# Attention and a gated feed-forward on one core: input products by blocks of seven, weights streamed from DRAM

## The chip, the cores and the metric

The kernel runs on one core of one Trainium2 chip. A core has TensorE (PE, with its weight loads shown apart as PEld), VectorE (DVE), ScalarE (ACT), GpSimd (POOL) and SyncE (SP), which here issues DMAs. The metric is the device time of one execution in microseconds; lower is better.

## The reference

```python
# q, k, v: (B=8, H=8, S=576, D=64); w_a, w_b: (512, 1536); w_out: (1536, 512); all float32
k_p = k.reshape(B, H, 72, 8, D).mean(axis=3)          # keys and values pooled by 8
v_p = v.reshape(B, H, 72, 8, D).mean(axis=3)
scores = (1 / sqrt(D)) * q @ k_p^T
attn = softmax(scores) @ v_p
x = attn.transpose(0, 2, 1, 3).reshape(4608, 512)     # one row a token
out = ((x @ w_a) * (x @ w_b)) @ w_out
```

## The kernel before

**Precision.** TensorE is given operands rounded to `fp32r`. To keep float32 accuracy each operand is split in a high part (a copy that rounds) and a low part (the rest, `low_part`, L172), and each product is three matmuls: high by high, high by low, low by high. The weights arrive as 64-bit words (`words`), which `convert_weights` turns into float32 with two ACT and three DVE operations a block (L212 to L223).

**Work.** The feed-forward runs over 9 tiles of 512 tokens (`NT`) and, in each, over 12 blocks of 128 hidden units (`f`). For a block `ffn_in` makes two products into PSUM (`psa`, `psb`; 4 blocks of the model width x 3 matmuls of 512 columns each, L549 to L551); ACT copies the first out (L554), DVE multiplies the second by it (L527), and the result is split (`hh`, `hl`). `ffn_out` multiplies it by `w_out` into four PSUM tiles `acc` (L570 to L572), which gather over all 12 blocks and are written out once a tile (L576, L578). The float32 weights stay in SBUF (`raw`, 72 KB in each partition); `split_weight` splits each block anew for every tile: one ACT copy (L235) and one low part, on DVE in tile 0 for `a` and `b`, on POOL otherwise.

**Attention** goes in 40 chunks of up to 128 tokens (`chunk`): load of queries, split, scores (L389 in the first `SUMMED` chunks, L403 and L406 later, with L409 adding two halves), softmax, split of the probabilities, transposes (L474) and, for a block of chunks, the product with the values (L507 to L510), whose result is split into `xh` and `xl`, the feed-forward's input.

**Order.** Nothing reorders at run time: each engine follows the order in which the program emits. `Chains` holds generators; each yields the number of steps until it goes on, or `PE` for a place between feed-forward matmuls. `ffn_in` and `ffn_out` call `chains.step()` between their groups, so attention, splits and conversions are laid between the products; `need` steps until something has been emitted. All DMAs go out on SP in program order, so a DMA that waits holds up those behind it.

Of the kernel before, what the change touches and what calls it, by code (L numbers as in the profile page):

```python
# [23 lines left out]
NT = 512  # L24
NTILE = B * S // NT
NF = DF // P
NK = DM // P


SHRINK = 2.0**-112  # L30
SCALE = 1.0 / float(D) ** 0.5
# [11 lines left out]


# [5 lines left out]
SLOTS = 6  # L50
TILE_SLOTS = SLOTS * NF

BLOCK, BLOCK_LATER = 256, 384

NTMP = 6

SUMMED = 9

AHEAD = 2

GROUPS = 4


SPLIT_A, SPLIT_B, SPLIT_O = 1, 4, 4
PROBS_GAP, VALUE_GAP = 2, 4
CHUNK, CHUNK_LATER, CHUNK_GAP = 34, 32, 10
KEYS_AHEAD, VALUES_AFTER = 18, 16


EARLY_GAP, VALUES_START, KEYS_START, WEIGHTS_START, CONVERT_AFTER = 1, 2, 4, 10, 5  # L70
# [3 lines left out]

# [35 lines left out]

@with_exitstack
def attn_moe_kernel(ctx: ExitStack, tc: tile.TileContext, q, k, v, vr, wa, wb, wo, out):
# [15 lines left out]
    raw = {name: const.tile([P, NF, 512], F32, name=f"w{name}_raw") for name in ("a", "b", "o")}
# [8 lines left out]
    work = sb.tile([P, 2 * NK * BLOCK_LATER], I32, tag="work", name="words", bufs=1)  # L140
    area = {name: work[:, x * 1024:(x + 1) * 1024] for x, name in enumerate(("a", "b", "o"))}

    flat = [(b, o, n) for b in range(B) for o, n in chunks_of(b)]
    tile_of = [(b * S + o) // NT for b, o, n in flat]
    early = sum(t == 0 for t in tile_of)

    blocks, start = [], 0

    def cut(chunks, limit):

        best = None
        for x in range(1, len(chunks) + 1):
            total = sum(flat[c][2] for c in chunks[:x])
            if total > limit:
                break
            cost, rest = cut(chunks[x:], limit) if x < len(chunks) else (0, [])
            cost += max(total, 2 * P)
            if best is None or cost < best[0]:
                best = cost, [chunks[:x]] + rest
        return best  # L160

    while start < len(flat):
        stop = start
        while stop < len(flat) and flat[stop][0] == flat[start][0] and tile_of[stop] == tile_of[start]:
            stop += 1
# [19 lines left out]
    def load_early():  # L185
# [7 lines left out]
        for i in range(2, early):  # L193
            load_raw_queries(i, early_q[:, i])
# [488 lines left out]
```

## Time and profile before

| | |
|---|---|
| runs | 1088.93, 1089.23, 1089.97 us; median 1089.23 |
| span of the profiled execution, first to last instruction | 1086.9 us; its whole time is not listed apart from the runs, and the median stands 2.3 us above the span |
| busy: PE, PEld, DVE, ACT, POOL | 1029.8, 856.0, 580.4, 523.3, 531.7 us |
| granted TensorE clock | 0.984 of full over the span |
| DMA | 59.58 MB, 55 GB/s on average |
| first feed-forward product, end of tile 0, of tile 1, start of the last tile | 58.6, 203, 313.4, 982.2 us |

Matmuls are pipelined, and a matmul's recorded duration overlaps the next one's: 512 columns are listed at 0.39 us and start 0.23 us apart. Rows of groups give line, engine, operation, output <- inputs, shapes and count, then busy us and mean ns of one, then idle time of the engine just before them and what ended it.

### The profile page before, as it was taken

How to read it: one execution, taken by the hardware profiler on the slowest of the kernel's cores; microseconds unless marked ns; L12 is line 12 of the kernel's file. 1: busy time of each engine (PE TensorE's matmuls, PEld its weight loads, DVE VectorE, ACT ScalarE, POOL GpSimd, SP SyncE). 2: the span in 40 equal slices, each digit the busy share in tenths (PEclk: the TensorE clock that was granted, in tenths of full speed). 3: DMA queues.
4: the chain of work that ended last, by engine and by line, in shares of the span. 5: the costliest groups of instructions: out<-in, count | busy, mean ns of one | idle time of the engine just before them, and what ended most of it. 6: DMA issues, size and time to landing. Idle time of an engine off the chain costs nothing.

```text
span 1086.9 us, 13596 instructions
## 1 busy us (share of the span) xinstructions
PE 1029.8 (95%) x4964; PEld 856.0 (79%) x4964; DVE 580.4 (53%) x941; ACT 523.3 (48%) x1051; POOL 531.7 (49%) x441
## 2 busy tenths in 40 slices
PE   4388779999999999999999999999999999999998
PEld 4277667888887888888888888888888888888886
DVE  8889998733476335733476436644457243322112
ACT  3666566544454445544455445444445344443332
POOL 6112322555545554665555555555546455555442
PEclk9779989999999999999999999999999999999999
DMA  6454453200121001400040003100221020001001
GB/s 222 134 157 129 134 169 110 89 23 1 56 84 46 2 3 44 129 1 1 22 131 1 1 1 120 55 1 1 73 73 30 1 68 1 1 1 39 1 1 39
DMA packets 29874, 59.58 MB, mean 55 GB/s; under 512 B 7121, under 2 KB 7121, under 8 KB 29809
## 3 DMA queue, kind: packets, MB, share of 16 engines
q1 hardware_dynamic: 29808, 58.73, 16.9%
q8 instruction: 39, 0.64, 0.2%
q14 instruction: 27, 0.21, 0.1%
HBM read 49.28 MB, written 9.44 MB: 54 GB/s over the span
## 4 chain that ended last, share of the span: by engine, by line
PE 84%; DVE 9%; ACT 3%; DMA 2%; issue 1%; POOL 0%; SPq 0%; DVEq 0%; ACTq 0%; POOLq 0%
PE acc L570 9%; PE psa L549 9%; PE acc L572 8%; PE psa L551 8%; PE acc L571 8%; PE psb L549 8%; PE psa L550 8%; PE psb L551 8%; PE psb L550 8%; PE ptr L474 3%; PE psc L403 2%; DVE wb_raw L218 1%; PE po L509 1%; PE po L510 1%; PE psc L406 1%
## 5 line engine op out<-in xcount | busy, mean ns | idle before, releaser
L527 DVE TENSOR_TENSOR h<-psb,h 128x512 f32<-128x512 f32 x108 | 74.5, 690 | 343.7 <-PE psb L551 326.6
L172 POOL TENSOR_TENSOR jlb<-wb_raw,jhb 128x512 fp32r<-128x512 f32 x96 | 125.6, 1309 | 218.2 <-ACT jhb L235 218.2
L172 POOL TENSOR_TENSOR jla<-wa_raw,jha 128x512 fp32r<-128x512 f32 x96 | 126.5, 1317 | 140.9 <-ACT jha L235 117.9
L172 POOL TENSOR_TENSOR jlo<-wo_raw,jho 128x512 fp32r<-128x512 f32 x108 | 154.2, 1428 | 82.4 <-ACT jho L235 74.8
L554 ACT COPY h<-psa 128x512 f32<-128x512 f32 x108 | 63.5, 588 | 234.7 <-PE psa L551 229.4
L570 PE MATMUL acc<-jho,hh 128*128 128x512 f32 x432 | 174.3, 404 | 0.0
L549 PE MATMUL psb<-xh,jhb 128*128 128x512 f32 x432 | 171.6, 397 | 1.9 <-DVE h L527 1.9
L549 PE MATMUL psa<-xh,jha 128*128 128x512 f32 x432 | 172.5, 399 | 0.0
L551 PE MATMUL psb<-xh,jlb 128*128 128x512 f32 x432 | 169.4, 392 | 0.1
L572 PE MATMUL acc<-jho,hl 128*128 128x512 f32 x432 | 169.3, 392 | 0.0
L551 PE MATMUL psa<-xh,jla 128*128 128x512 f32 x432 | 169.2, 392 | 0.0
L550 PE MATMUL psa<-xl,jha 128*128 128x512 f32 x432 | 169.2, 392 | 0.0
L571 PE MATMUL acc<-jlo,hh 128*128 128x512 f32 x432 | 169.1, 391 | 0.0
L550 PE MATMUL psb<-xl,jhb 128*128 128x512 f32 x432 | 168.9, 391 | 0.0
L530 ACT CAST hh<-h 128x512 fp32r<-128x512 f32 x108 | 67.1, 622 | 76.7 <-DVE h L527 76.7
L172 DVE TENSOR_TENSOR hl<-h,hh 128x512 fp32r<-128x512 f32 x108 | 91.6, 848 | 20.8 <-ACT hh L530 20.6
L551 PEld LDWEIGHTS psb<-xh,jlb 128*128 128x128 f32 x432 | 81.6, 189 | 18.0 <-DVE jlb L172 0.6
L551 PEld LDWEIGHTS psa<-xh,jla 128*128 128x128 f32 x432 | 81.7, 189 | 17.7
L572 PEld LDWEIGHTS acc<-jho,hl 128*128 128x128 f32 x432 | 81.4, 188 | 17.7
L549 PEld LDWEIGHTS psb<-xh,jhb 128*128 128x128 f32 x432 | 81.5, 189 | 17.5 <-issue 2.3
L429 POOL TENSOR_TENSOR s<-s,z 128x576 f32<-128x576 f32 (+1 forms) x38 | 52.3, 1376 | 86.3 <-DVE z L427 48.8
L549 PEld LDWEIGHTS psa<-xh,jha 128*128 128x128 f32 x432 | 81.7, 189 | 15.3
(91 smaller groups left out, 1721.6 us busy)
## 6 DMA issues: line engine op xcount, KB each, us to landing
out<-y SPq DMA_DIRECT2D x36, 256.0 KB, 2.2
kraw<-in_k SPq DMA_DIRECT2D x28, 288.0 KB, 3.5
vraw<-in_v SPq DMA_DIRECT2D x28, 256.0 KB, 3.0
qraw<-in_q SPq DMA_DIRECT2D x28, 256.0 KB, 3.7
words<-in_wa SPq DMA_DIRECT2D x12, 512.0 KB, 3.6
words<-in_wb SPq DMA_DIRECT2D x12, 512.0 KB, 3.5
words<-in_wo SPq DMA_DIRECT2D x12, 512.0 KB, 3.6
vraw<-in_vr SPq DMA_DIRECT2D x14, 192.0 KB, 2.6
```

The costliest lines, as they stand in the source:

```text
L172: eng.tensor_tensor(out=lo, in0=src, in1=hi.bitcast(F32), op=ALU.subtract)
L429: (nc.vector if first and i % 2 else nc.gpsimd).tensor_tensor(out=s[:n], in0=s[:n], in1=z[:n].unsqueeze(2).broadcast_to([n, H, SP]), op=AL ...
L474: nc.tensor.transpose(ptr[:rows, g, :n], src, ident[:n, :n])
L527: nc.vector.tensor_tensor(out=h, in0=pt, in1=h, op=ALU.mult)
L530: nc.scalar.copy(hh, h)
L549: nc.tensor.matmul(pt, wh[:, c], xh[:, kk], start=(kk == 0), stop=False)
L550: nc.tensor.matmul(pt, wh[:, c], xl[:, kk], start=False, stop=False)
L551: nc.tensor.matmul(pt, wl[:, c], xh[:, kk], start=False, stop=(kk == NK - 1))
L554: nc.scalar.copy(h, pt)
L570: nc.tensor.matmul(acc[c], hh[:, cs], wh, start=(f == 0), stop=False)
L571: nc.tensor.matmul(acc[c], hh[:, cs], wl, start=False, stop=False)
L572: nc.tensor.matmul(acc[c], hl[:, cs], wh, start=False, stop=(f == NF - 1))
```

## The change

**Blocks of seven.** Tokens are taken in pairs of halves of 384 (`HB`): 6 pairs of 768. Pair 0 is done as before, with matmuls of 384 columns. From pair 1 on, `block` takes a pair of hidden blocks (`j`: hidden blocks 2j and 2j+1), the two halves of the model width and the two token halves as 2x2 matrices and makes the product from seven block products instead of eight (`PRODUCTS7`), for `w_a` and `w_b` (m = 0, 1) each. Products gather in four PSUM banks, X and Y for each matrix; between products that use the same bank ACT copies a partial result out (`snap`) or DVE adds it to one taken before (`combine`). The left factors are parts of the weights or sums of them (S1 to S4), the right ones blocks of x or sums of them (T1 to T4).

**Weights.** They no longer stay in SBUF. While pair 0 runs, each block is converted (two ACT and two DVE operations now; the words are loaded from ACT's DMA queue), split once, used, and its parts stored to DRAM (`keep`), the float32 block too. `block_sums` loads that back, makes the four sums on POOL, splits and stores them. From then on `load_parts` streams each item's seven left factors and two blocks of `w_out` from DRAM, 512 KB each, into rings of SBUF buffers (`own`, `stream`, `raws`, `outs`). A `Ring` hands out a buffer only when the program has emitted the last use of its earlier content.

**Output.** `outer` makes the output product of one item (two hidden blocks) into one of two PSUM tiles; `taken_outer` copies the first into SBUF and adds the later ones there with DVE. Items of pair 0 are ordered so that j = 0, 1 come first for half 0 alone, then j = 2 to 5 for both halves, then j = 0, 1 for half 1 (`LEAD` = 2).

**Attention** of pair p + 1 is spread over the items of pair p and leaves x unsplit in `xraw`; `prepare` forms and splits the seven right factors while the last item of pair p goes through. The early steps take three chunks instead of four, and the shorter score path holds for 14 chunks instead of 9.

The diff, cut to its core:

```diff
-NT = 512
+NJ = NF // 2
+HB = 384
+NP = 2 * HB
+PRODUCTS7 = (
+    ("A11", "B11", "X", True), ("A12", "B21", "Y", True), ("S2", "T2", "X", False), ("S1", "T1", "Y", True),
+    ("S3", "T3", "X", False), ("S4", "B22", "Y", False), ("A22", "T4", "X", False),
+)
-SUMMED = 9
+SUMMED = 14
+BLOCK_STEPS = 20
+raws = Ring(sb, "raw", 3, [P, 2, 512], F32)
+own = Ring(sb, "we", 4, e_shape, F32R)
+stream = Ring(sb, "ws", 4, e_shape, F32R)
+outs = Ring(sb, "wo", 4, [P, 2, 512], F32R)
+gates = Ring(sb, "h", 7, [P, HB], F32)
+gated = Ring(sb, "hh", 6, [P, 2, HB], F32R)
+    def keep(key, e, ring, after=STORE_AFTER):
+        yield after
+        kept[key] = dr.tile([P, 1024], F32, name="kept_%s_%s" % key)
+        nc.sync.dma_start(kept[key], flat_e.bitcast(F32))
...
+            nc.scalar.activation(w, hi.bitcast(F32), AF.Copy, scale=SHRINK)
+            nc.scalar.activation(low, lo.bitcast(U32), AF.Copy, scale=LOW_BITS)
+            if f + 2 < NF:
+                load_words(f + 2)                      # nc.scalar.dma_start
-            nc.vector.tensor_scalar(...); nc.vector.scalar_tensor_tensor(...); nc.vector.tensor_tensor(...)
+            nc.vector.scalar_tensor_tensor(
+                out=low, in0=wi, scalar=3, in1=low, op0=ALU.logical_shift_left, op1=ALU.bitwise_or)
+            nc.vector.scalar_tensor_tensor(
+                out=wi, in0=wi, scalar=-(1 << 31), in1=low, op0=ALU.bitwise_and, op1=ALU.bitwise_or)
+    def split_inner():
...
+                nc.scalar.copy(e[:, 0], src)
+                low_part((nc.vector, nc.gpsimd)[h], e[:, 1], src, e[:, 0])
+                chains.start(keep((f, h), e, None), LATER, 1)
+            chains.start(keep(("raw", f), rawt[f], raws), LATER, 1)
+    def block_sums(j):
...
+            nc.sync.dma_start(r[-1].rearrange("p m c -> p (m c)"), kept["raw", f])
+        for name, a, b, op in (S1, S2, S4, S3):
+            nc.gpsimd.tensor_tensor(out=t, in0=a, in1=b, op=op)
+            while not own.can():
+                yield 1
+            e = own.take((j, name))
+            nc.scalar.copy(e[:, 0], t)
+            low_part(nc.gpsimd, e[:, 1], t, e[:, 0])
+            chains.start(keep((j, name), e, own), LATER, 1)
+    def load_parts():
+        while len(loaded) < len(wanted) and wanted[len(loaded)] in kept:
+            x = len(loaded)
+            ring = stream if x < first_block else (own, stream)[x % 2] if x < first_third else (own, stream, raws)[x % 3]
+            if not ring.can():
+                break
+            e = ring.take(x, e_shape, F32R)
+            nc.sync.dma_start(e..., kept[wanted[x]])
+    def block(item):
+        for x, (left, right, bank, opens) in enumerate(PRODUCTS7):
+            need(lambda: len(loaded) > taken["i"] and ("operand", p, right) in done)
+            for m in range(2):
+                need(lambda: ("read", name) in done or (name, "open") not in done)
+                for kk in range(2):
+                    nc.tensor.matmul(pt, e[:, 0, m, c], xo[:, 0, kk], start=(opens and kk == 0), ...)
+                    nc.tensor.matmul(pt, e[:, 0, m, c], xo[:, 1, kk], ...)
+                    nc.tensor.matmul(pt, e[:, 1, m, c], xo[:, 0, kk], ...)
+                chains.start(taken_block(item, x, m, pt, name, snaps), PRODUCTS, 1)
+                step()
+            if x: yield                                # once for each m; one group of outer() goes here
+        # taken_block: snap = ACT copy of the bank to SBUF; combine = DVE add of bank and snap, then for m = 1
+        # POOL multiplies the two matrices' results, ACT rounds, POOL makes the low part
+    def outer(item):
+        for half in halves(item):                      # (1, 0)
+            for c in range(HB // P):
+                pt = ps.tile([P, DM], F32, tag="acc", bufs=2)
+                for y in range(2): three matmuls of 512 columns
+    def taken_outer(item, row, tokens, pt):
+        if opens: nc.scalar.copy(acc[row], pt)
+        else: nc.vector.tensor_tensor(out=acc[row], in0=pt, in1=acc[row], op=ALU.add)
+items = [("n", (0,), j) for j in range(LEAD)] + [("n", (0, 1), j) for j in range(LEAD, NJ)]
+items += [("n", (1,), j) for j in range(LEAD)] + [("s", p, j) for p in range(1, NPAIR) for j in range(NJ)]
+        for x in range(NJ):
+            chains.start(behind(begins["s", 1] + (x - 2) * BLOCK_STEPS, block_sums(x)), LATER)
```

More of the change, by code (lines that the diff above doesn't have):

```diff
@@ new lines, in split_outer @@
+    def split_outer():
+        for f in range(NF):
+            yield from wait(("weight", "o", f))
+            while not outs.can() or order_o[next_o[0]] != ("own", f):
+                yield 1
+            next_o[0] += 1
+            e = outs.take(("own", f))
+            w = rawt.pop(("o", f))
+            nc.scalar.copy(e[:, 0], w)
+            yield 1
+            low_part(nc.gpsimd, e[:, 1], w, e[:, 0])
+            tmps.give(("o", f))
+            parts["o", f] = e
+            chains.start(keep(("o", f), e, None), LATER, 1)
+            yield 2
@@ new lines, in attn_moe_kernel, with step, need, finish @@
+    taken = {"i": 0, "o": 0}
+    def step(groups=1):
+        chains.step(groups)
+        load_parts()
+    def need(ready):
+        n = 0
+        while not ready():
+            step(GROUPS)
+            n += 1
+            assert n < 2000
+    acc = {}
+    gs = {}
+    def finish(key, f, half, h):
+        while not gated.can():
+            yield 1
+        e = gated.take((key, f, half))
+        nc.scalar.copy(e[:, 0], h)
+        yield 1
+        low_part(nc.gpsimd, e[:, 1], h, e[:, 0])
+        gates.give((key, f, half))
+        gs[key, f, half] = e
@@ new lines, in taken_outer @@
+    def taken_outer(item, row, tokens, pt):
+        j = item[2]
+        opens, closes = j == 0, j == NJ - 1
+        if item[0] == "n" and row >= HB // P:
+            opens, closes = j == LEAD, j == LEAD - 1
+        if opens:
+            acc[row] = sb.tile([P, DM], F32, tag=f"acc{row}", name=f"y_{tokens}", bufs=1)
+            nc.scalar.copy(acc[row], pt)
+        else:
+            nc.vector.tensor_tensor(out=acc[row], in0=pt, in1=acc[row], op=ALU.add)
+        if closes:
+            yield 1
+            nc.sync.dma_start(out[tokens:tokens + P, :], acc[row])
+        else:
+            return
+            yield
@@ new lines, in attn_moe_kernel, with behind @@
+        need(lambda: have(0) and ("parts", 0) in done)
+        begins, starts, at = {}, [], 0
+        for item in items:
+            begins.setdefault(item[:2], at)
+            starts.append(at)
+            at += BLOCK_STEPS if item[0] == "s" else 11 * len(item[1])
+        def behind(when, chain):
+            x = max(y for y in range(len(starts)) if starts[y] <= when)
+            yield from wait(("item", x))
+            if when > starts[x]:
+                yield when - starts[x]
+            yield from chain
@@ L638 @@
+        step()
+        step()
+        for _ in before:
+            step()
+        for _ in range(4):
+            step()
 _OUTS = [((B * S, DM), "float32")]
```

675 lines of the change are left out of this document (477 added, 198 removed).

## The prediction

> **What bounds the kernel now.** I read the page's engine shares first, then the table of windows cut at the first product and at the borders of token tiles, then single matmuls in the timeline.
>
> ```profile
> span 1086.9 us, 13596 instructions
> ...
> PE 1029.8 (95%) x4964; PEld 856.0 (79%) x4964; DVE 580.4 (53%) x941; ACT 523.3 (48%) x1051; POOL 531.7 (49%) x441
> ...
> PE 84%; DVE 9%; ACT 3%; DMA 2%; issue 1%; POOL 0%; SPq 0%; DVEq 0%; ACTq 0%; POOLq 0%
> ...
> 0.00:58.60 58.60, 25.57 (x120) 23.18 (x121) 48.35 (x83) 28.56 (x61) 23.00 (x33) 0.87 0.56 182
> 58.60:203.00 144.40, 124.19 (x589) 99.59 (x588) 131.19 (x211) 89.01 (x177) 38.85 (x29) 0.94 0.41 129
> 203.00:313.40 110.40, 110.40 (x537) 92.70 (x536) 50.65 (x86) 52.02 (x105) 59.84 (x48) 1.00 0.12 41
> 313.40:982.20 668.80, 668.80 (x3279) 557.35 (x3279) 329.83 (x535) 319.76 (x649) 366.98 (x298) 1.00 0.11 35
> 982.20:1086.90 104.70, 100.84 (x445) 83.15 (x444) 20.34 (x28) 33.90 (x61) 42.97 (x34) 1.00 0.06 21
> ```
>
> The window columns are PE, PEld, DVE, ACT, POOL, then granted clock, DMA share, GB/s. There are two kernels in one. Until 203 us (attention of tile 0, then tile 0's products beside the weight conversion) DVE is busy 131.2 of 144.4 us: DVE is the limit. From 203 us PE never pauses and the others are half idle; six tiles take 668.8 us, 111.5 each. How dense PE is there the timeline says (start, duration):
>
> ```profile
> 316.16 0.39 PE L549 MATMUL psb<-xh,jhb 128*128 128x512 f32 x1
> ...
> 318.65 0.39 PE L551 MATMUL psb<-xh,jlb 128*128 128x512 f32 x1
> ...
> 718.73 0.34 PE L507 MATMUL po<-p,vdiag 128*128 128x384 f32 x1
> 718.90 0.34 PE L508 MATMUL po<-p,vdiag 128*128 128x384 f32 x1
> 719.09 0.34 PE L509 MATMUL po<-p,vdiag 128*128 128x384 f32 x1
> 719.26 0.34 PE L510 MATMUL po<-p,vrem 96*128 96x384 f32 x1
> 719.44 0.40 PE L570 MATMUL acc<-jho,hh 128*128 128x512 f32 x1
> ```
>
> Start to start, 11 matmuls of 512 columns take 2.49 us, 0.2265 each; four of 384 take 0.71, 0.1775 each, with a weight load for each matmul as everywhere. Three quarters of 0.2265 is 0.170: the narrower matmul is not held up by its weight load, it pays 0 to 0.0075. I take 0.176. A tile's 432 products of 512 columns are 97.9 us, so attention costs PE 13.6 a tile.
>
> **Steady part: block items.** An item is 768 tokens by 256 of the hidden width, both matrices. Before, that is 72 matmuls of 512 columns: 16.3 us. After, 7 products x 2 matrices x 6 matmuls of 384: 84 x 0.176 = 14.8. Saved 1.5 an item, 46 over 30 items (bounds 43 to 61). Pair 0 stays unblocked but at 384: 96 x 0.176 = 16.9 an item, 0.6 lost, 3.5 in six. The output products stay 36 x 0.2265 = 8.2 an item. So an item is 23.0 us, a pair 138, with attention for the next pair (1.5 x 13.6) 158.
>
> The Trainium skill, "TensorE: Matmul & The Clock Gate", section "Back-to-back issue gap", gives N/2.4 + 2.5 ns for warm matmuls, so 162.5 and 215.8 ns for these widths. By it the estimate is 56 us saved over 30 items instead of 46; the rows above are 5 to 9% slower than the page, and I go by the rows.
>
> What an item adds elsewhere is priced by these groups (busy, mean ns):
>
> ```profile
> L527 DVE TENSOR_TENSOR h<-psb,h 128x512 f32<-128x512 f32 x108 | 74.5, 690 | 343.7 <-PE psb L551 326.6 <-PE ptr L474 6.2 <-ACT qh L358 6.0
> ...
> L172 DVE TENSOR_TENSOR xl<-po,xh 128x384 fp32r<-128x384 f32 x16 | 8.9, 554 | 7.8 <-ACT xh L518 7.8
> ...
> L518 ACT CAST xh<-po 128x384 fp32r<-128x384 f32 x16 | 7.7, 478 | 16.9 <-PE po L510 16.9
> ...
> L172 POOL TENSOR_TENSOR jlo<-wo_raw,jho 128x512 fp32r<-128x512 f32 x108 | 154.2, 1428 | 82.4 <-ACT jho L235 74.8 <-DVE jla L172 7.6
> ...
> L172 POOL TENSOR_TENSOR jlb<-wb_raw,jhb 128x512 fp32r<-128x512 f32 x96 | 125.6, 1309 | 218.2 <-ACT jhb L235 218.2
> L172 DVE TENSOR_TENSOR hl<-h,hh 128x512 fp32r<-128x512 f32 x108 | 91.6, 848 | 20.8 <-ACT hh L530 20.6
> ...
> L235 ACT CAST jho<-wo_raw 128x512 fp32r<-128x512 f32 x108 | 67.2, 622 | 0.0
> ...
> 605.32 0.39 PE L551 MATMUL psa<-xh,jla 128*128 128x512 f32 x1
> ...
> 605.75 0.59 ACT L554 COPY h<-psa 128x512 f32<-128x512 f32 x1 [1.20 <-PE psa L551]
> ```
>
> DVE: seven combinations out of PSUM at 0.554 and, because an output product no longer stays in PSUM over twelve hidden blocks but is added up in SBUF after each item, six additions at 0.690: 8.0 an item, 48 a pair. Attention on DVE is 55 a tile less 12 x (0.690 + 0.848) for gates, 36, so 54 a pair; preparing the next pair's operands (4 sums, 4 low parts of 768 columns) 9. Sum 111 of 158, 70%, against 49% before. ACT: 53 a tile less 36 splits at 0.622 and 24 gate copies at 0.6 leaves 16 for attention, 24 a pair; eleven copies at 0.48 an item, 32; seven 768-wide copies and six first output rows, 10: 66 of 158. POOL: seven ops of about 1.07 (three quarters of 1.428), 45 a pair, plus attention (367/6 less 36 splits at 1.36, the mean of the two rows, = 12 a tile, 18) and three low parts of 768 columns, 6: 69 of 158. No engine passes PE on average. What is tight is order. The X bank that product 7 leaves is opened again by the next item after only six matmuls, 1.06 us, and the copy must read it between: 0.2 from the matmul's end to the copy's start (an estimate: 605.75 - 605.32, less the 0.2265 that the matmul streams) and 0.48, or 0.55 on DVE. An engine inside another op then makes PE wait 0.3 to 0.6. The output product also waits for DVE, POOL, ACT and POOL in a row (0.55 + 1.07 + 0.5 + 1.07, before hops) in a 5.2 us space. I charge 0.7 an item, 4 a pair (bounds 0 and 2.5).
>
> **Streams.** Per item SP issues seven block loads and two output-weight loads, 512 KB each, 4.7 MB; with q, k, v and results 222 GB/s through the pair. SP's own time, about 0.4 per issue by the chain's two rows below, is 3.6 of 26 us. A load that waits for a buffer to be freed holds up the q, k, v loads and the result stores behind it on SP, and attention would wait for them; query chunks start 34 steps early (an item is 20), so nothing is charged.
>
> ```profile
> 0.74 0.37 SPq L183
> 1.16 0.42 SPq L188
> ...
> words<-in_wo SPq DMA_DIRECT2D x12, 512.0 KB, 3.6
> ...
> 0.00:27.00 27.00, 12.96 (x56) 11.86 (x56) 22.04 (x38) 9.37 (x20) 18.29 (x28) 1.00 0.67 221
> ...
> 135.00:162.00 27.00, 21.20 (x105) 17.44 (x104) 25.20 (x43) 16.93 (x34) 6.45 (x5) 0.88 0.51 163
> ```
>
> 221 GB/s at share 0.67 and 163 at 0.51 both extrapolate to some 325: 222 is 68% of it, with up to 11 buffers (1.6 items) ahead. Hidden.
>
> **Pair 1** has the block sums besides: per item four sums and four low parts on POOL, 8 x 1.36 = 11, four copies on ACT, two reloads and four stores on SP. POOL goes to 45 + 18 + 6 + 65 = 134 of 158, 85%, and a sum has to be made, stored and reloaded (3.6 each way) before its product. Its buffers come from the ring that the loads also use. No row shows such a chain; bounds 0 and 60 for the pair, I take 12, nearer the first since each chain starts two items ahead.
>
> **Start.** To the end of pair 0, three engines compete.
>
> ```profile
> L223 DVE CUSTOM_DVE_ANT_0 wb_raw<-wb_raw,wlow_b 128x1024 uint16<-128x1024 uint16 x12 | 11.7, 971 | 1.5
> L218 DVE SCALAR_TENSOR_TENSOR wb_raw<-words,wb_raw 128x512 int32<-128x512 int32 x12 | 11.3, 943 | 0.2
> ...
> L214 DVE TENSOR_SCALAR wb_raw<-wb_raw 128x512 int32<-128x512 int32 x12 | 6.3, 522 | 2.9 <-ACT wb_raw L212 2.9
> ...
> L172 DVE TENSOR_TENSOR jlb<-wb_raw,jhb 128x512 fp32r<-128x512 f32 x12 | 8.2, 681 | 0.0
> ...
> L409 DVE TENSOR_REDUCE s<-psc 128x144 f32<-128x288 f32 x100 | 41.1, 451 | 54.0 <-PE psc L406 53.6
> L374 DVE TENSOR_TENSOR s<-s,m 128x576 f32<-128x576 f32 x25 | 28.3, 1133 | 0.9
> ...
> L373 DVE TENSOR_REDUCE m<-s 128x8 f32<-128x576 f32 x25 | 18.8, 752 | 0.8
> ...
> L374 DVE TENSOR_TENSOR s<-psc,m 128x288 f32<-128x288 f32 x14 | 6.4, 457 | 0.9
> L373 DVE TENSOR_REDUCE m<-psc 128x4 f32<-128x288 f32 x14 | 6.3, 448 | 0.4 <-PE psc L389 0.4
> ```
>
> DVE did 48 + 131 us of work until 203, and half of 51 more until 768 tokens were through, at about 258: 205. Three conversion ops become two of L218's kind: about 0.55 x 36 = -20. Half of the 24 early low parts (0.68 to 0.77) and 18 gate low parts (0.848) leave for POOL: -9, -15. 30 output additions: +21. 256 more tokens of attention must be done by then: +18. Five more chunks take the shorter score path, 2 x (0.457 + 0.448) instead of 4 x 0.451 + 1.133 + 0.752, and pair 1's x gets no low part there: -11. Preparation +9. Sum 198; at the 91% of before, 218. PE: first product at about 53 (58.6 before, with four chunks instead of three ahead of it), 101 + 49 us of products, 30 of attention: 233. DMA: 12 x 7 transfers of 512 KB (three words, four stores) and 6 MB of inputs, 50 MB at 325 GB/s, 154 us in the 190 there are; words are now issued on ACT (36 x 0.4, hidden in 60% use). Three limits this close add waits: I take 245 (bounds 228 and 270).
>
> **Sum.** 245, pair 1 158 + 4 + 12, pairs 2 to 4 3 x 162, pair 5 (no attention behind it) 142, end 3.8 as now plus 3 for the last output product, which has nothing to cover its chain: 1056 of span. The profiled execution's span is 1086.9; the median run shown is 1089.2, 2.3 around it. Forecast 1058.
>
> **Rivals.**
> 1. All ends good: start at 230, stalls half, pair 1 free: 1058 - 15 - 10 - 12 - 5 = 1016. For it: the steady trace stands still almost nowhere. Against: 70% DVE.
> 2. Ends slower: POOL sets pair 1. The chain of one j is 4 x (1.4 + 0.6 + 1.4) plus reload and store 7, and with 12 of other POOL ops in the same queue comes to some 33 us against the 26 an item takes. Priced at 8 an item instead of 2: +36, 1094; it decides from 7 lost per item. For: 85%, one queue. Against: two items of lead.
> 3. Ends slower: DVE or ACT late at the banks in each item, 2.5 instead of 0.7: +54, 1112. L172's 848 against L527's 690 shows DVE ops on SBUF already stretched beside POOL.
> 4. Streamed transfers don't overlap: 9 x 3.6 = 32.4 per item, 9.4 over the 23 of the last pair and 6.4 over the others, some 200 more, 1255. Against: 512 KB in 3.6 us is 146 GB/s and 221 was seen on the same queue.
> 5. The gain is eaten: 1089.
>
> The Trainium skill, "DMA: Bandwidth & Descriptors", section "Measured (HBM→SBUF, 128 partitions, SWDGE, issued from GpSimd)", asks for 1 MiB a transfer and its fit gives 2.0 us + bytes/436e3, an estimated 3.2 for 512 KB; transfers taken singly would then give 29 us an item, near rival 4. The 221 GB/s row speaks against that reading.
>
> **How the numbers follow.** Forecast 0.50 (own range 1030 to 1080), rival 1 0.18, rival 2 0.13, rival 3 0.11, rival 4 0.05, rival 5 0.03. Rivals 2 and 3 are spread around the old time, a quarter of each faster: faster 0.74, same 0.03, slower 0.23, where 0.2% (2.2 us) is what this measurement can tell. Leaving out rival 4 and the tails of 1 and 3, 1010 to 1115.
>
> **What would show it.** Right: the seven products' matmuls 0.175 apart; items of about 23.5 us in the last pair; POOL near 85% in pair 1 and 45% after; DMA near 220 GB/s in pairs 2 to 5; the first blocked product near 245. Wrong: PE idle behind X or Y banks over 1.5 us an item, block loads waited for by PE, or pair 1 above 185 us.

## The result and the profile after

The change makes the kernel slower: 1123.03 us (median of 4 runs, 1119.69 to 1125.40) against 1089.08 (4 runs on the same chip, 1087.75 to 1089.97), a ratio of 1.0308 [1.0283, 1.0334]. Forecast were 1058 us and a range from 1010 to 1115. The profiled execution has a span of 1119.4 us.

From the page of the changed kernel: span, engine totals, traffic, shares of the chain that ended last, and three groups.

```profile
span 1119.4 us, 15231 instructions
...
PE 1013.6 (91%) x5424; PEld 931.8 (83%) x5424; DVE 638.4 (57%) x1067; ACT 466.7 (42%) x1006; POOL 503.0 (45%) x462
...
HBM read 203.42 MB, written 47.19 MB: 224 GB/s over the span
...
PE 59%; DVE 15%; DMA 13%; ACT 5%; POOL 3%; issue 3%; SPq 1%; ACTq 0%; POOLq 0%; DVEq 0%
...
L975 DVE TENSOR_TENSOR y<-acc_s,y 128x512 f32<-128x512 f32 x150 | 102.9, 687 | 134.8 <-PE acc_s L952 134.5
...
L894 DVE TENSOR_TENSOR h<-psYA,h 128x384 f32<-128x384 f32 x60 | 33.2, 554 | 65.8 <-PE psYA L870 58.7
...
L899 POOL TENSOR_TENSOR h<-h,h 128x384 f32<-128x384 f32 x90 | 98.1, 1090 | 231.5 <-DVE h L894 213.6
```

PE is 16 us less busy than before, and the span is 32.5 us longer: PE fell from 84% of the chain to 59%, and DMA rose from 2% to 13%. The new operations cost what the prediction paid for them (0.687 for 0.690, 0.554 for 0.554, 1.09 for 1.07).

Windows of the changed kernel, cut at the first product, the first blocked product, the first matmul of each later pair, and the end (us; busy PE, PEld, DVE, ACT, POOL; clock, DMA share, GB/s):

```profile
0.00:62.60 62.60, 24.78 (x110) 20.97 (x111) 46.25 (x79) 30.25 (x64) 29.46 (x37) 0.99 0.65 216
62.60:294.30 231.70, 199.14 (x1055) 183.35 (x1055) 158.64 (x246) 126.19 (x262) 105.73 (x88) 0.90 0.70 249
294.30:476.80 182.50, 165.16 (x877) 151.51 (x876) 101.12 (x177) 77.56 (x170) 117.43 (x100) 0.94 0.78 277
476.80:643.60 166.80, 160.11 (x885) 146.35 (x883) 97.45 (x169) 65.71 (x148) 66.38 (x64) 1.00 0.59 213
643.60:811.60 168.00, 160.32 (x870) 148.14 (x871) 99.78 (x171) 67.84 (x150) 69.74 (x66) 0.98 0.61 214
811.60:968.60 157.00, 157.00 (x880) 145.82 (x879) 85.21 (x149) 64.33 (x142) 68.96 (x66) 1.00 0.58 201
968.60:1119.40 150.80, 147.06 (x757) 135.62 (x755) 49.96 (x80) 34.79 (x73) 45.33 (x45) 1.00 0.50 178
```

| term | forecast | measured | difference |
|---|---|---|---|
| to the first blocked product | 245 | 294.3 | +49 |
| pair 1 | 174 | 182.5 | +8.5 |
| pairs 2 to 4 | 486 | 491.8 | +6 |
| pair 5 and the end | 149 | 150.8 | +2 |
| around the span | 2.3 | 3.6 (median 1123.0 less 1119.4; the profiled execution itself took 1121.2) | +1 |

The forecast column adds up to 1056, not to the 1058 on record; more on that below. Three quarters of the miss lie in the start. The kernel before had 768 tokens through at about 258, in this row of its windows:

```profile
58.60:258.00 199.40, 179.19 (x858) 145.69 (x857) 157.50 (x253) 115.28 (x228) 70.18 (x54) 0.95 0.34 106
```

Beside the row 62.60:294.30 this says the most. DVE's work is the same (157.5 and 158.6), ACT has 11 us more and POOL 36, and yet the stretch is 32 us longer. DVE's busy share goes from 79% to 68%, and no other engine is near full but PE, whose busy time grew by 20 and whose idle time grew from 20 to 33.

What PE's time there consists of is worked out from the starts of all its matmuls: a start-to-start distance up to columns/2.4 + 13 ns (173 at 384, 226 at 512) counts as work, distances doubled by the half clock as slow clock, the rest as a gap ahead of the next group. (The rows add up to their stretches within half a us.)

| us | products | attention | half clock | gaps ahead of attention | gaps ahead of products |
|---|---|---|---|---|---|
| before, 58.6 to 258 | 144.4 | 16.8 | 7.3 | 23.9 | 7.5 |
| after, 62.6 to 294.3 | 144.6 | 23.3 | 16.0 | 38.5 | 9.7 |

The gaps stand ahead of attention's matmuls. Waits of PE in 62.6 to 294.3 of the changed kernel (total us, times, longest):

```profile
PE ptr L598 <- ACT turned L599: 12.4, 6, 4.6
PE ptr L598 <- DVE xB L209: 5.3, 1, 5.3
PE psc L524 <- DVE ql L209: 4.9, 3, 2.1
PE ptr L598 <- DVE s L509: 3.1, 2, 1.8
```

PE stands at transposes and scores for ACT and DVE, and the products emitted behind a waiting matmul wait with it.

What lies behind these waits is told by the chain of work that ended last, cut to the two stretches and, for comparison, to the same stretch of f2 below, which leaves most of the conversion out (us of the chain on each engine):

| | PE | DVE | ACT | DMA | POOL | issue |
|---|---|---|---|---|---|---|
| before, 58.6 to 258 | 80.9 | 77.5 | 23.5 | 3.0 | 2.6 | 11.5 |
| after, 62.6 to 294.3 | 85.0 | 70.2 | 38.9 | 17.2 | 5.7 | 12.1 |
| f2, 53.1 to 265.8 | 116.7 | 38.0 | 16.2 | 28.6 | 4.3 | 6.7 |

Of the 32 us, 15 are ACT's, 11 of them in the copies that convert the weights (8.0 before, 18.7 after), and 14 are DMA's, almost all of it loads of values that a reduction waits for (`vraw`: 3.0 before, 15.0 after). POOL's added work is hardly on the chain.

### The profile page after: what moved, and what is told of

It is laid out like the page before. It is cut to its first block, busy times and chain, and to the rows that moved or that the text cites. A ratio compares the mean times of both kernels' runs of the same rounds, so it can differ in the third digit from the quotient of the medians.

```text
span 1119.4 us, 15231 instructions
## 1 busy us (share of the span) xinstructions
PE 1013.6 (91%) x5424; PEld 931.8 (83%) x5424; DVE 638.4 (57%) x1067; ACT 466.7 (42%) x1006; POOL 503.0 (45%) x462
## 4 chain that ended last, share of the span: by engine, by line
PE 59%; DVE 15%; DMA 13%; ACT 5%; POOL 3%; issue 3%; SPq 1%; ACTq 0%; POOLq 0%; DVEq 0%
PE acc_s L950 6%; PE acc_s L952 6%; PE acc_s L951 6%; DMA kept_S<-we 4%; PE psXA L868 3%; PE psXB L868 3%; PE psXA L870 3%; PE psXA L869 3%; PE psXB L869 3%; PE psXB L870 3%; DMA vraw<-in_vr 3%; DMA vraw<-in_v 2%; PE psYA L868 2%; PE psYB L868 2%; PE psYA L869 2%
## 5 line engine op out<-in xcount | busy, mean ns | idle before, releaser
L209 POOL TENSOR_TENSOR hh<-h,hh 128x384 fp32r<-128x384 f32 x144 | 150.6, 1052 | 128.6 <-ACT hh L905 80.8
L899 POOL TENSOR_TENSOR h<-h,h 128x384 f32<-128x384 f32 x90 | 98.1, 1090 | 231.5 <-DVE h L894 213.6
L975 DVE TENSOR_TENSOR y<-acc_s,y 128x512 f32<-128x512 f32 x150 | 102.9, 687 | 134.8 <-PE acc_s L952 134.5
L950 PE MATMUL acc_s<-wo,hh 128*128 128x512 f32 x360 | 144.8, 402 | 2.6 <-ACT y L973 2.6
L951 PE MATMUL acc_s<-wo,hh 128*128 128x512 f32 x360 | 142.8, 397 | 0.0
L952 PE MATMUL acc_s<-wo,hh 128*128 128x512 f32 x360 | 142.7, 396 | 0.0
L888 ACT COPY h<-psXA 128x384 f32<-128x384 f32 x90 | 43.1, 479 | 125.2 <-PE psXA L870 125.1
L952 PEld LDWEIGHTS acc_s<-wo,hh 128*128 128x128 f32 x360 | 68.2, 189 | 15.9
L950 PEld LDWEIGHTS acc_s<-wo,hh 128*128 128x128 f32 x360 | 68.3, 190 | 11.4 <-ACT y L973 2.9
L951 PEld LDWEIGHTS acc_s<-wo,hh 128*128 128x128 f32 x360 | 68.3, 190 | 8.3
L905 ACT CAST hh<-h 128x384 fp32r<-128x384 f32 x90 | 45.5, 515 | 58.6 <-POOL h L899 58.2
L599 ACT CAST turned<-ptr 128x512 fp32r<-128x512 f32 (+1 forms) x80 | 43.2, 544 | 55.8 <-PE ptr L598 53.7
L209 POOL TENSOR_TENSOR pr<-s,pr 128x512 fp32r<-128x512 f32 (+1 forms) x40 | 52.9, 1323 | 25.2 <-ACT pr L572 19.5
L544 DVE TENSOR_REDUCE s<-psc 128x144 f32<-128x288 f32 (+1 forms) x104 | 42.7, 449 | 36.3 <-PE psc L541 36.2
```

Source lines behind the costliest of these rows:

```text
L209: eng.tensor_tensor(out=lo, in0=src, in1=hi.bitcast(F32), op=ALU.subtract)
L899: nc.gpsimd.tensor_tensor(out=t, in0=t, in1=a, op=ALU.mult)
L905: nc.scalar.copy(e[:, 0], t)
L950: nc.tensor.matmul(pt, e[:, 0, cs], wos[y][:, 0], start=(y == 0), stop=False)
L951: nc.tensor.matmul(pt, e[:, 0, cs], wos[y][:, 1], start=False, stop=False)
L952: nc.tensor.matmul(pt, e[:, 1, cs], wos[y][:, 0], start=False, stop=(y == 1))
```

## The experiments

Times are medians in us, with the ratio to the kernel before on the same chip; the last columns are read off the starts of matmuls in each trace.

| run | total | ratio to before | first product | first blocked | pair 1 | 2 | 3 | 4 |
|---|---|---|---|---|---|---|---|---|
| the change | 1123.03 | 1.0308 [1.0283, 1.0334] | 62.6 | 294.3 | 182.5 | 166.8 | 168.0 | 157.0 |
| e1 | 1124.28 | 1.0322 [1.0300, 1.0345] | 61.5 | 290.8 | 185.2 | 166.0 | 165.9 | 161.6 |
| e6 | 1119.69 | 1.0266 [1.0235, 1.0296] | 61.4 | 291.7 | 182.9 | 166.8 | 166.7 | 159.2 |
| f1 | 1121.91 | 1.0310 [1.0286, 1.0335] | 69.8 | 302.9 | 179.2 | 162.4 | 166.4 | 157.1 |
| e5 | 1103.75 | 1.0127 [1.0109, 1.0144] | 57.8 | 278.0 | 181.7 | 164.9 | 163.7 | 159.5 |
| e8 | 1102.60 | 1.0118 [1.0094, 1.0141] | 56.1 | 272.5 | 186.4 | 167.0 | 164.8 | 159.3 |
| f2 | 1096.15 | 1.0072 [1.0054, 1.0091] | 53.1 | 265.8 | 183.6 | 167.0 | 166.7 | 162.4 |
| e2 | 1112.32 | 1.0215 [1.0183, 1.0248] | 61.7 | 295.0 | 173.8 | 164.9 | 160.2 | 162.2 |
| e4 | 1112.88 | 1.0205 [1.0170, 1.0239] | 60.8 | 293.6 | 179.5 | 163.0 | 165.1 | 162.2 |
| e7 | 1109.27 | 1.0188 [1.0170, 1.0206] | 62.3 | 294.6 | 171.2 | 166.4 | 166.1 | 158.2 |
| e9 | 1115.70 | 1.0253 [1.0223, 1.0284] | 61.8 | 301.4 | 172.6 | 163.8 | 160.3 | 162.8 |
| e10 | 1109.46 | 1.0182 [1.0167, 1.0197] | 55.8 | 299.8 | 180.1 | 160.8 | 158.7 | 157.2 |
| e11 | 1145.56 | 1.0529 [1.0502, 1.0556] | 63.7 | 302.4 | 184.6 | 171.8 | 164.8 | 164.3 |
| e13 | 1134.12 | 1.0402 [1.0368, 1.0436] | 62.9 | 300.1 | 179.5 | 169.3 | 168.8 | 164.3 |
| e12 | 1137.96 | 1.0443 [1.0428, 1.0459] | 61.1 | 285.7 | 174.9 | 172.7 | 168.2 | 169.5 |
| f3 | 1092.21 | 1.0037 [1.0021, 1.0053] | 62.7 | 292.6 | 167.0 | 161.3 | 158.7 | 157.1 |
| f4 | 1097.09 | 1.0079 [1.0058, 1.0101] | 61.4 | 299.0 | 167.1 | 161.2 | 158.6 | 157.2 |
| f5 | 1086.12 | 0.9965 [0.9951, 0.9979] | 61.2 | 290.1 | 163.6 | 160.5 | 158.8 | 157.1 |
| f9 | 1090.04 | 1.0011 [1.0002, 1.0020] | 61.4 | 296.2 | 164.9 | 160.4 | 158.2 | 157.0 |

### The start: is it the stores?

**e1.** The parts of pair 0 are not stored, but for the first f's.

```diff
+        same = ("o", 0) if key[0] == "o" else ("raw", 0) if key[0] == "raw" else (0, key[1])
+        if not isinstance(key[1], str) and key != same:
+            kept[key] = kept[same]
...
+            return
         kept[key] = dr.tile(...)
```

> Leaves out 47 of the 48 kinds of stores of pair 0 and of the block sums beyond the first of each kind (later loads read the first one's copy, so the results are not the reference's); every load, conversion, split and sum stays. Changed kernel: first blocked product at 294.3 us, 1123 us in all. Theory stores (the 25 MB of stores in pair 0 fill the DMA queue and hold up words, keys and values): first blocked product at 255 to 265, total about 1090. Theory order (attention of the second half is due too early, in-order engines wait for one another): 285 to 294, total 1112 to 1123. Theory DVE work: no change, 290 to 294.

Contrary to that text the 24 stores of the block sums stayed in; 44 of pair 0's 48 went. Its window of the start:

```profile
61.50:290.80 229.30, 194.84 (x1054) 178.79 (x1054) 159.06 (x247) 126.21 (x262) 105.72 (x88) 0.93 0.47 152
```

249 GB/s became 152 and the stretch lost 2.4 of 231.7 us. The stores are not what makes the start long.

### The start: is it when attention is due, or what the weights' conversion costs?

**e6.** The items on both halves of pair 0 read half 0's operands for half 1 and don't wait for half 1.

```diff
-                need(lambda: all(have(u) for u in item[1]))
+                need(lambda: all(have(u) for u in item[1] if len(item[1]) == 1 or u == 0))
...
-                    xs = xop["half", u]
+                    xs = xop["half", 0 if len(us) > 1 else u]
```

> The four items of pair 0 for both halves use half 0's operands for half 1 as well and do not wait for half 1's attention (results are not the reference's); that attention is still done, as is all other work. Theory order (half 1's attention, due after two items, holds PE up): the item that took 41 us takes about 25, first blocked product at 275 to 280, total about 1105. Theory engine latency (PE's path runs through DVE and ACT whatever the due time, since conversion and attention share their queues): the wait moves to a later item, first blocked product at 288 to 294, total 1115 to 1123.

2.6 us at the first blocked product. The item after the first one on both halves begins at 149.8 instead of 152.7, and the next at 190.0 instead of 192.8, though that first one began at 115.0 instead of 126.9: the wait moved behind, it was not half 1's due time.

**f1.** More steps between attention's stages, so that PE meets each result later.

```diff
-PROBS_GAP, VALUE_GAP = 2, 4
-CHUNK = 34
+PROBS_GAP, VALUE_GAP = 5, 7
+CHUNK = 42
```

> Attention's groups on PE are emitted three steps later after the work that feeds them (gaps of 5 and 7 steps instead of 2 and 4), and chunks begin 8 steps earlier to match; same work. In the changed kernel PE stands 38.5 us ahead of attention groups between 62.6 and 294.3 us. Theory placement (the groups are emitted too close behind DVE and ACT work): the 38.5 falls to about 20, first blocked product at 270 to 275, total about 1095. Theory supply (what feeds them is not done earlier, wherever PE waits for it): first blocked product at 290 to 300, total 1115 to 1130.

The gaps ahead of attention fell from 38.5 to some 29 us, those ahead of products rose from 9.7 to some 19 (two of them, of 7.4 and 5.4 us, stand ahead of output products), and the stretch is as long as it was (233.1). Spacing the order out moved the waits here and removed none.

**e5, e8, f2.** Conversion work is taken out step by step: e5 the first scalar_tensor_tensor of each conversion; e8 also ACT's copy of the low word, but for f = 0; f2 both scalar_tensor_tensors and that copy.

```diff
-            nc.vector.scalar_tensor_tensor(
-                out=low, in0=wi, scalar=3, in1=low, op0=ALU.logical_shift_left, op1=ALU.bitwise_or)
...
-            nc.scalar.activation(low, lo.bitcast(U32), AF.Copy, scale=LOW_BITS)
```

> Leaves out the first of the two DVE operations that convert a weight block, 36 operations of about 0.75 us, 27 us of DVE in pair 0 (results are not the reference's). Theory DVE work (DVE bounds pair 0): first blocked product 20 to 27 us earlier, about 270, total about 1098. Theory order: half of that or less, 282 to 292, total about 1113 to 1121. Theory stores: no change.

> Leaves out the first DVE operation and the second ACT operation of each weight block's conversion but the first: about 27 us of DVE and 20 us of ACT less in pair 0 (results are not the reference's). DVE alone gave the first blocked product at 278.0 against 294.3. Theory engine latency (path alternates between DVE and ACT): 265 to 270, total about 1092. Theory DVE alone: 276 to 278, total 1103. Theory order: 275 to 278.

> Leaves out both DVE operations and the second ACT operation of every weight block's conversion (results are not the reference's): some 55 us of DVE and 20 us of ACT less in pair 0. The first DVE operation alone gave the first blocked product at 278.0, with the ACT operation 272.5, against 294.3. Theory supply (each us of DVE or ACT work that feeds attention is some 0.5 us of PE's wait): 250 to 258, total about 1085. Theory placement: 268 to 273 again, total about 1100.

The first blocked product comes 16.3, 21.8 and 28.5 us earlier; of these 4.8, 6.5 and 9.5 lie before the first product already. The window after it, of f2:

```profile
53.10:265.80 212.70, 190.06 (x1054) 175.81 (x1053) 111.45 (x187) 109.91 (x232) 101.16 (x88) 0.94 0.75 272
```

DVE has 47 us less to do here than in the change (111.5 for 158.6) and ACT 16 less (109.9 for 126.2), and the stretch is 19.0 shorter. The 265.8 lies between what the two theories expected. Step by step, the first 23 us of DVE (e5) shorten the stretch by 11.5, ACT's 16 (e8) by another 3.8, and the second 24 us of DVE (f2) by 3.7. So conversion is on the path, but less of it the more is taken out, and it is not the whole: with DVE at 52% PE still has 26.0 us of gaps ahead of attention and 8.4 of half clock (e5: 30.3 and 12.6; e8: 28.3 and 10.5). Were DVE alone the limit, each us taken out would give near 1 us.

What comes to the fore is the loads of values: they are 15.0 us of the chain in the change, 29.6 in e8 and 28.6 in f2. In e10 and f4 below, where they are asked for earlier, none is left on the chain of the start, but stores and reloads of weight blocks come in their place (15.2 and 20.4 us), and the first blocked product is not earlier. No run takes conversion out and asks for the inputs earlier at once.

### Pair 1: sums, their stores and the loads behind them

Of the changed kernel, a piece of the chain in pair 1 (start, us, what) and PE's waits there:

```profile
444.62 1.31 POOL we L209
...
445.95 5.75 DMA kept_S<-we
...
451.71 3.31 DMA ws<-kept_S
...
455.16 0.66 PE psXA L868
```

```profile
PE psXA L868 <- DMA ws<-kept_S: 9.0, 2, 5.8
...
PE psXA L868 <- ACT h L888: 1.8, 1, 1.8
PE psXB L868 <- DVE h L927: 1.2, 1, 1.2
```

This sum's store takes 5.75 us, SP stands at the reload until it has landed, and the reload takes 3.31: about 9 us where the prediction had 7.2. PE waits 5.8 us for it. After it PE runs slow for a while (start, duration):

```profile
455.94 0.52 PE L870 MATMUL psXA<-xT,ws 128*128 128x384 f32 x1
456.26 0.52 PE L868 MATMUL psXA<-xT,ws 128*128 128x384 f32 x1
...
461.70 0.34 PE L869 MATMUL psYA<-xT,we 128*128 128x384 f32 x1
461.87 0.34 PE L870 MATMUL psYA<-xT,we 128*128 128x384 f32 x1
```

Matmuls of 384 columns start 0.32 apart until 459.1 and those of 512 columns behind them 0.42 apart until 460; then the 384 are 0.17 apart. The Trainium skill, "TensorE: Matmul & The Clock Gate", section "What's actually happening", has half the clock after an idle window of about 3.4 us and the full one back after as long a busy one; the trace agrees in kind (5.8 us of idling, 4.9 us of slow matmuls behind).

**e2.** `LEAD` from 2 to 4: four items of pair 0 take half 0 alone first, and as many items on half 1 alone stand ahead of pair 1, which gives the sums more work in front.

```diff
-LEAD = 2
+LEAD = 4
```

> LEAD 4 instead of 2: four items of pair 0 for half 0 alone before half 1 is needed, then two for both, then four for half 1 with reloaded weights (16 block loads and 8 output-weight loads instead of 8 and 4). Theory order: the 41 us item before the first item of both halves shrinks, first blocked product at about 270, total about 1098. Theory stores: more reloads on the same queue, first blocked product at 294 or later, total 1123 to 1130. Theory DVE work: half 0 alone gives PE less to do for each converted block, 294 or later.

The start does not move (295.0), against the 270 that the theory of order expected; pair 1 is 8.7 us shorter.

**e4, e7.** In both, the loads of the sums are replaced by loads of A11; e7 also stores only j = 0's sums.

```diff
-            wanted += [names.get(a, (j, a)) for a, *_ in PRODUCTS7]
+            wanted += [names.get(a, (2 * j, 0)) for a, *_ in PRODUCTS7]
...
-            chains.start(keep((j, name), e, own), LATER, 1)
+            if j == 0: chains.start(keep((j, name), e, own), LATER, 1)
+            else: chains.start(give_later(own, (j, name)), LATER, 1)
```

> Items load A11's parts where they should load S1 to S4, so no load waits for a block sum; the sums are still made, split and stored, and as many bytes are loaded (results are not the reference's). Changed kernel: pair 1 182.5 us, pair 5 147. Theory late sums (the chain sum, store, reload is late in pair 1): pair 1 about 165, total about 1106. Theory POOL or DMA load in pair 1: pair 1 stays at 178 to 183, total about 1121. The first blocked product stays near 294 in both.

> As the run with plain loads, and the block sums of j = 1 to 5 are made and split but not stored: 20 stores of 512 KB fewer, as a rule in pair 1 (results are not the reference's). Pair 1 was 182.5 us in the changed kernel and 179.5 with plain loads. Theory DMA (SP stands behind the sums' stores, and queues are near full): pair 1 at 163 to 168, total about 1100. Theory POOL (the sums' 11 us an item on POOL): pair 1 at 176 to 180, total about 1112.

Pair 1 in e4 and e7, same columns as above:

```profile
293.60:473.10 179.50, 162.87 (x877) 149.81 (x876) 104.70 (x177) 76.73 (x169) 115.64 (x100) 0.94 0.77 275
```

```profile
294.60:465.80 171.20, 159.97 (x878) 146.49 (x876) 103.32 (x178) 75.72 (x167) 110.59 (x96) 0.97 0.63 223
```

Not having to wait for the sum that is being stored gives 3 us, taking the stores away 8 more. (e7 also gives the sums' buffers back without waiting for a store, so the 8 are not the queue's alone.) POOL has nearly the same work in both (115.6, 110.6) as in the change (117.4): it was not POOL's work that set the pair. 14 us over the 157 of pair 4 remain.

**e9.** `LEAD` 4, and a stored part may be loaded only six steps after its store was issued, so that SP should not stand at a reload.

```diff
-        kept[key] = dr.tile(...)
+        place = dr.tile(...)
...
+        yield LAND
+        kept[key] = place
```

> LEAD 4, and a stored part counts as there for the loads only six steps after its store is issued (a sum's buffer is given back then too), so SP does not stand at a load that waits for the store to land. With LEAD 4 alone: pair 1 173.8 us, total 1112. Theory DMA (SP standing behind stores in pair 1): pair 1 at 163 to 168, total about 1103. Theory POOL: pair 1 at 172 to 178, total 1110 to 1116.

In pair 1 SP still stands 20.2 us at reloads of sums (33.3 in e2, 48.0 in the change). Pair 1 is 1.2 us better than in e2, the start 6 worse: no gain, and no test of a queue that never stands.

### Pairs 2 and 3: attention's own inputs

q, k, v are asked for on SP's queue between the block loads. Issue to landing before (first fence) and after (size, median us at the end of the row):

```profile
kraw<-in_k SPq DMA_DIRECT2D x28, 288.0 KB, 3.5
vraw<-in_v SPq DMA_DIRECT2D x28, 256.0 KB, 3.0
qraw<-in_q SPq DMA_DIRECT2D x28, 256.0 KB, 3.7
```

```profile
kraw<-in_k SPq DMA_DIRECT2D x28, 288.0 KB, 6.3
tmp<-in_q SPq DMA_DIRECT2D x29, 256.0 KB, 6.4
vraw<-in_v SPq DMA_DIRECT2D x28, 256.0 KB, 4.1
```

**e10.** All of them are asked for earlier, and the reductions that read them stand further behind.

```diff
-                yield 4    # keys; values 3 -> 8, queries 5 -> 9
+                yield 9
...
-CHUNK = 34
-KEYS_AHEAD, VALUES_AFTER = 18, 16
+CHUNK = 38
+KEYS_AHEAD, VALUES_AFTER = 40, 26
```

> Keys, values and queries are asked for four or five steps longer before DVE or ACT use them (9, 8 and 9 steps instead of 4, 3 and 5), and the chains begin earlier to match; same work. Value loads land in 4.1 us (reduced rows of the remainder 4.2) against 3.0 and 2.6 before, beside 225 GB/s, and DVE stands in order until they do. Theory input latency (these waits hold DVE and then PE): first blocked product at 280 to 285, pair 1 at 172, pairs 2 and 3 at 162, total about 1092. Theory compute queues (DVE and ACT work, not loads): 290 to 296, pair 1 180, total 1115 to 1125.

Pair 2 goes from 166.8 to 160.8, pair 3 from 168.0 to 158.7, where PE hardly stands:

```profile
640.70:799.40 158.70, 158.09 (x871) 147.48 (x871) 95.31 (x166) 65.65 (x143) 70.00 (x66) 0.99 0.61 218
```

This is at the same rate (218 GB/s, 214 in the change): the transfers do hide, but DVE's reduction had been queued for an input that lands in 4 to 6 us as if it took 3. DVE's waits for inputs in pairs 2 and 3, the change first (476.8 to 811.6, 479.9 to 799.4):

```profile
DVE vp L432 <- DMA vraw<-in_vr: 8.0, 3, 6.1
DVE vp L432 <- DMA vraw<-in_v: 3.5, 2, 3.1
DVE tmp L375 <- DMA kraw<-in_k: 1.5, 1, 1.5
```

```profile
DVE vp L432 <- DMA vraw<-in_v: 1.8, 1, 1.8
```

Values land no sooner in e10 (5.1 us for 4.1); it is the reader that has room. Single pairs vary by several us from run to run of different edits (pair 3 is 160.2 in e2 without this one), but the sum of pairs 2 to 4 separates them: 476 to 477 us in the five runs with earlier inputs from pair 2 on (e10, f3, f4, f5, f9), 486 to 496 in the other runs of the seven products that leave the inputs on SP. In the start the same edit brings the first product forward by 6.8 us and the first blocked one back by 5.5.

**e11, e13.** The input loads are issued on ACT instead; e13 with `LEAD` 4 besides.

```diff
-                nc.sync.dma_start(kraw[j], ...)
+                nc.scalar.dma_start(kraw[j], ...)
```

> Loads of keys, values and later queries go out on ACT's DMA queue, not on SP's behind the weight stream and the stores; same work, about 96 issues more on ACT at 0.33 us and their waits for buffers on ACT. Theory input latency: landings fall towards 3 us, total 1095 to 1110, unless ACT's waits for free buffers give it back. Theory compute queues: no gain, 1120 to 1135 by the issues on ACT.

> LEAD 4 and inputs on ACT's DMA queue together. If both gain by themselves and independently: 1112 less what the queue alone gains, 1085 to 1100. If the loads were not the cause: 1110 to 1125.

q lands in 4.0 us instead of 6.4 and k in 5.3 instead of 6.3, but v in 5.4 instead of 4.1, and the kernel loses 22 us (22 also in e13 against e2). The Trainium skill, "DMA: Bandwidth & Descriptors", section "Issuing engines are not separate DMA queues", says that another issuing engine saves its sequencer's time alone. The trace agrees in that nothing was gained over all; by kind of load, two landed sooner and one later. Where the loss comes from is not shown: ACT stands some 17 us ahead of these loads, issuing takes it 54.6 us instead of 12.7, and values land later.

### What the seven products are worth

**e12.** The same streaming with eight plain products: four loads an item, no sums, two gate buffers fewer.

```diff
-            wanted += [names.get(a, (j, a)) for a, *_ in PRODUCTS7]
+            wanted += [(2 * j + y, h) for y in range(2) for h in range(2)]
...
-(normal if item[0] == "n" else block)
+(normal if item[0] == "n" else eight)
```

> Pairs 1 to 5 by eight plain block products with the same streaming: four left factors an item instead of seven, four right factors instead of seven, no block sums, no stored float32 blocks, five gate buffers instead of seven. 96 matmuls of 384 columns an item instead of 84: 24.9 us an item instead of 23.1 where nothing waits (pair 5), 54 us over 30 items. DMA falls to about 120 GB/s in pairs 2 to 5. Theory of seven as the gain (the scheme saves its 54 us less what the sums cost in pair 1): pair 1 about 172, pairs 2 to 4 about 170, total 1140 to 1150. Theory of the stream as the cost (without 7 loads an item and sums, pair 0 and pair 1 lose their waits): first blocked product at 275 to 285, pair 1 at 170, total 1120 to 1130.

```profile
801.50:971.00 169.50, 169.50 (x949) 158.42 (x949) 68.30 (x123) 53.01 (x116) 45.42 (x45) 1.00 0.37 129
```

An item of the last pair takes 25.2 us with eight products and 23.1 with seven: 2.1 an item, 63 over 30. Of the 63, the totals show 15 (1137.96 against 1123.03). The seven-product kernel gives back 8.6 until the first blocked product (it has raw parts to store, two items' sums to make and more operands to prepare there; which of them costs it is not shown) and 7.6 in pair 1; pairs 2 and 3 gain 5.9 and 0.2 instead of 12.6 each, and only pair 4, with 12.5, and pair 5 gain it whole.

The run says something else as well: with eight plain products the streamed kernel is 49 us slower than the one before (1137.96 for 1089.39). That is the price of the other parts of the change together; the seven products win 15 of it back.

### Putting the gains together

f3: `LEAD` 4, and e10's earlier inputs only from batch 3 and pair 2 on. f4: also for batch 2 and pair 1. f5 and f9: f3 with `LEAD` 5 and 6 (in f9 attention for pair 1 is spread from 11 steps ahead of half 1's items on, and the first operands of pair 1 are prepared from half 0's last item on). The edit of f5:

```diff
-LEAD = 2
+LEAD = 5
...
-                yield 4
+                yield 9 if b >= 3 else 4
...
-                begin_at = max(0, end - CHUNK)
+                begin_at = max(0, end - (CHUNK if p == 1 else 38))
...
-                    keys_at = max(0, begin_at - KEYS_AHEAD)
+                    keys_at = max(0, begin_at - (40 if b + 1 >= 3 else KEYS_AHEAD))
```

> A version: LEAD 4, and inputs from batch 3 and pair 2 on asked for earlier, pair 0 and 1 as in the changed kernel. LEAD 4 alone: pair 1 173.8 us, 1112 in all; earlier inputs alone: pairs 2 to 4 160.8, 158.7, 157.2. If the two add up: first blocked product 295, pair 1 174, pairs 2 to 4 477, total about 1098. If the gains of pairs 2 and 3 came from the earlier state and not from the inputs: total 1110.

> As the version with LEAD 4 and earlier inputs (1092.2 us, first blocked product 292.6), and the inputs of batch 2 and pair 1 too are asked for earlier, in pair 0. Theory inputs (value loads are on PE's path in pair 0 as they were in pairs 2 and 3): first blocked product at about 284, total about 1083. Theory supply (DVE and ACT work is the path there): 290 to 296, total 1090 to 1096.

> As the version with LEAD 4 and earlier inputs, with LEAD 5: five items for half 0 alone, one for both, five for half 1 with reloaded weights. Theory order with more time for half 1: pair 1 about 170, first blocked product 290, total about 1087. Theory nothing more to gain (half 1 was early enough with four, one more item of reloads costs): total 1092 to 1098.

> As the version with LEAD 5 and earlier inputs (1086.1 us, ratio 0.9965 to the kernel before; first blocked product 290.1, pair 1 163.6), with all six items of pair 0 first for half 0 and then for half 1: half 1's attention is needed only after the last conversion, and every weight block is reloaded once more. Theory order with more time for half 1: first blocked product at 285 to 288, total about 1082. Theory nothing more to gain: 1086 to 1092, since the conversion then has only half of a block's products beside it.

The gains add up: f3 came in 6 us under the 1098 of its sum, and f5 beats both kernels, by a third of a percent the one before (0.9965 [0.9951, 0.9979]). Its windows:

```profile
61.20:290.10 228.90, 199.11 (x1054) 181.40 (x1053) 160.99 (x249) 128.34 (x266) 110.63 (x92) 0.91 0.83 299
290.10:453.70 163.60, 157.89 (x878) 145.12 (x876) 104.93 (x174) 75.64 (x168) 111.09 (x97) 0.99 0.86 306
453.70:614.20 160.50, 158.42 (x886) 146.56 (x884) 100.43 (x176) 66.66 (x152) 67.44 (x65) 1.00 0.63 226
```

From pair 1 on it takes 790.8 us (1080.9 less 290.1), against 809 forecast for that part (174 + 486 + 149). f5 has 1086.12 us (1082.36 to 1086.84) against 1088.87. The first blocked product stays between 290 and 295 in e1, e2, e4, e6, e7, f3 and f5; f4, at 299.0, says that earlier inputs don't help there, and f9 that a sixth item of lead gives nothing more.

## Why the prediction was wrong

- **The sum.** Its terms add up to 1053.8 us of span, not 1056, and to 1056.1 with the 2.3 around it, not 1058. The slip of 2 us changes nothing below.
- **Item and matmul sizes: right.** 23.0 us forecast, 23.1 measured for the last pair's items; 384-column matmuls 175 ns apart for 176. Pair 4, with its attention, took 157.0 for 158 + 4.
- **Stalls at the banks, rival 3: not seen.** In all of pair 1, PE's waits at X and Y banks for ACT and DVE are 3.0 us; the 4 us charged per pair for them were not needed in pair 4 at all. Its 1112 lies near the result for a cause that did not come.
- **Streams, rival 4: right that they overlap,** at 178 to 277 GB/s. **Wrong that they cost nothing:** landing times rose from 3.0-3.7 to 4.1-6.4 us, and reductions queued for the old times made pairs 2 and 3 6 and 9 us longer. "Query chunks start 34 steps early" covered less than it seemed to, since keys and values are not queries and the reader is queued in order. That the sum over pairs 2 to 4 was only 6 off is partly luck: the 4 us a pair charged at the banks stayed away.
- **Pair 1: 182.5 for 174.** POOL at 64% (117 of 182), not 85%: two of the six items' sums are begun in pair 0. Rival 2 is wrong: the pair lost 4.1 an item over 158, not 8, and e7 shortens it with POOL's work nearly unchanged. Of its 24.5 over 158, `LEAD` 5 with the inputs of pair 2 asked for earlier (the attention that runs beside pair 1) takes away 19. e7 puts 11 on the sums' stores and reloads, the sooner return of their buffers included.
- **Start: the failed step.** "Three limits this close add waits: I take 245" puts 12 us of waits on the largest of three totals, PE's 233 (first product at 53, 150 of products, 30 of attention). Measured are a first product at 62.6, 144.6 of products, 23.3 of attention, and 64.2 of gaps and half clock. PE's work was 12 us less than forecast, its first product 9.6 later, and its waits were 52 us more: together the 49 by which 245 became 294.3. That makes the sign wrong: with 245, the other measured terms would have come to 1074. Waits of this kind were there to be counted: the old kernel has 38.7 us of them from 58.6 to 258. The late first product goes with the conversion: without it (f2) it comes at 53.1. Of the signs of being wrong that were named beforehand, only block loads that PE waits for came true (9.3 us in pair 1), and none of those was about the start.
- **The other two totals of the start.** DVE's was right, 204.9 us until 294.3 (46.25 + 158.64) for 198. Its time was not: "at the 91% of before, 218" takes the share of the stretch in which DVE had been the limit, while until 258 it had been busy 205.9, 80%, and is busy 70% now. DMA moved some 71 MB until 294.3 (216 and 249 GB/s in the two rows) for the 50 forecast, which left out half 1's reloads among others; e1, with 48 MB, shows that this did not make the start long.
- **Open.** Why the waits are so many is shown in part. Attention for 768 tokens, conversion and products alternate between PE, DVE and ACT in one order; conversion is on the path (e5, e8, f2), its stores (e1), half 1's due time (e6) and the spacing (f1) are not, and the waits bring 16.0 us of half clock with them, 7.3 before. Of the start's 38.5 us of gaps ahead of attention, 26.0 stay in f2 with nearly no conversion. Late values are a part of them by f2's chain, and so may be attention's own steps from scores over exponentials and transposes to values, too short of other work between them; no run separates the two. What the sums' preparation costs in the start is bounded only by e12's 8.6.

## What to carry to other kernels

Where several engines hand work to each other in a fixed order, the largest total is a floor for the time, not the time. Work out the stretch from its last comparable windows as a whole, and count what the bounding engine waited there: 38.7 us of PE's gaps and half clock in the old start were a better first guess for the new one than 12, and still less than the 64.2 that came. DVE's overall share alone would not have warned: 198 us at 80% are 248. Let only a steady stretch with one full engine go by that engine's total. Price a new stream also by what its queue does to the transfers already there: each reader that was placed for the old landing time needs new room, and that was worth 15 us here (pairs 2 to 4 in e10), as much as the new stream's own waits (11 in e7). When a change shows little of an ideal gain, splitting the span at the same work in both kernels finds the debtor at once.

## What the runs showed of the hardware

- On one queue, transfers of 256 to 288 KB that landed in 3.0 to 3.7 us beside 55 GB/s took 4.1 to 6.4 beside 224 (medians; both rates are averages over the span).
- 512 KB transfers reached 306 GB/s over 163.6 us (f5, pair 1) at a DMA share of 0.86, and the pair beside it took 163.6 us, against 157.1 for pair 4 of the same run at 199 GB/s.
- A 5.8 us wait of PE cost about another 2 us (an estimate): for 4.9 us after it, matmuls of 384 columns stood 0.32 apart instead of 0.17, those of 512 columns 0.42 instead of 0.23.
